# Attention product folded into the output weight, with the inverse denominators broadcast by DMA

## The chip, the cores and the metric

The kernel runs on one core of a Trainium2 chip. The metric is the device time of one execution in microseconds (us), as a median over several executions. "Span" is the time from the first to the last instruction in a profiled execution, about 2 us less than the device time.

The engines are called as in the profile: PE is TensorE's matmul, PEld its weight load, DVE is VectorE, ACT is ScalarE, POOL is GpSimd, SP is SyncE, and SPq is the queue of DMA instructions that SP issues. PSUM is the memory of the tiles that PE's matmuls write, such as `acc_t`. The granted clock is the share of its full clock that PE was given; 1.00 is full.

## The reference, cut to what matters

```python
def _A_ref(x, wqkv, wo):                      # S = 2048, D = 1024, 32 heads of 32
    q, k, v = ...                             # from x @ wqkv, split in heads
    phi = lambda t: jnp.where(t > 0, t + 1, jnp.exp(t)) + 1e-6
    pq, pk = phi(q), phi(k)
    kv = jnp.einsum("bhsd,bhse->bhde", pk, v)             # 32 x 32 per head
    z = jnp.einsum("bhsd->bhd", pk)
    num = jnp.einsum("bhqd,bhde->bhqe", pq, kv)
    den = jnp.einsum("bhqd,bhd->bhq", pq, z)[..., None] + 1e-6
    return (num / den).transpose(...).reshape(B, S, D) @ wo

h = x + _A_ref(_layernorm(x), A_wqkv, A_wo)
h2 = h + _B_ref(_layernorm(h), ...)           # the "mixer": two large products over S, 2048 -> 3584 -> 2048
```

Everything up to `h` takes the first 235 us of the kernel before. The mixer takes the rest, and the change does not touch its arithmetic.

## The kernel before

The stage in question has three parts. "Query units" compute q for 128 columns and 512 rows at a time and apply phi. Between them, for every block of 128 rows, numerator and denominator come from eight small products, are divided, and are transposed by DMA. Then the output projection multiplies with `wo`. Its PSUM tiles are not started at zero: ScalarE first copies the residual `x` into the tile (the "seed"), and PE accumulates on top.

```python
pin = tc.keep_in_program_order                # otherwise the compiler orders each engine's instructions
...
def attn_num_den(i):
    for j in range(ND):                       # ND = 8; L1118, PE
        nc.tensor.matmul(nd_ps[...], lhsT=pqT[:, j, i*P:(i+1)*P], rhs=ndrhs[:, j, :], start=True, stop=True)
    dn = ...; nc.scalar.activation(dn, nd_ps[...], ACT.Ln, bias=eps_den[:])      # L1126
    rd = ...; nc.scalar.activation(rd[:], dn[:], ACT.Exp, scale=-1.0)            # L1134
    for b in range(NNB):
        nc.vector.tensor_tensor(o_sb[...], nd_ps[...], rd[...], ALU.mult)        # L1139
    return o_sb

def attn_transpose(i, o_sb):
    nc.sync.dma_start_transpose(out=pqT[:, :, i*P:(i+1)*P], in_=o_sb[:])         # L1148
...
def load_xr(i):                               # residual rows, 4 tiles; SP queue
    xr = xrpool.tile([P, D], BF16, name="xr")
    nc.sync.dma_start(xr[:], x[i*P:(i+1)*P, :])                                  # L1154
    xrs[i] = xr

def out_proj(i):                              # i = 0..15, two halves of 512 columns
    ...
    for dc in range(NDC):
        ap_ = acc_tile()                      # ring of 5 PSUM tiles
        nc.scalar.copy(ap_[:, 0:CW], xr[:, dc*CW:(dc+1)*CW])                     # L1165, seed, ACT
        for j in range(ND):
            nc.tensor.matmul(ap_[:, 0:CW], lhsT=pqT[:, j, i*P:(i+1)*P], rhs=wo_sb[:, j, ...], ...)   # L1167
        nc.scalar.copy(h_bf[:, ...], ap_[:, 0:CW])                               # L1177, evacuation, ACT
        nc.vector.bn_stats(st[:, dc, :], ap_[:, 0:CW])                           # L1178, DVE
    nc.vector.bn_aggr(mv_all[:, i, :], st[:])
    nc.scalar.activation(lnv[:], mv_all[:, i, 1:2], ACT.Ln, ...)                 # L1181, statistics, ACT
    nc.scalar.activation(sc_all[:, i:i+1], lnv[:], ACT.Exp, scale=-0.5)          # L1182
    nc.sync.dma_start(h_dram[i][:], h_bf[:])
```

None of the instructions of `out_proj` is pinned: the compiler chooses the order in which ACT takes seeds, evacuations and statistics.

Of the kernel before, what the change touches and what calls it, by code (L numbers as in the profile page):

```python
# [27 lines left out]
def kernel(  # L28
# [28 lines left out]
    NCOL = P + HB  # L57
    JPB = BANK // NCOL
    NNB = (ND + JPB - 1) // JPB
# [40 lines left out]
    for q in range(HB):  # L100
        nc.vector.memset(maskbd[q * DH:(q + 1) * DH, q * DH:(q + 1) * DH], 1.0)
        nc.vector.memset(m4[q * DH:(q + 1) * DH, q:q + 1], 1.0)
# [5 lines left out]
    nc.vector.memset(eps_den[:], DEN_EPS)  # L108
# [27 lines left out]
    def load_w1(u, half):  # L136
        if half == 0:
            w1_tiles[u] = w_tile(wpool, WLEN)[:, 0:NS * CW].rearrange("p (k f) -> p k f", f=CW)
        k = slice(half * NSP, (half + 1) * NSP)
        nc.sync.dma_start(  # L140
            w1_tiles[u][:, k, :],
            B_w1[:, u * CW:(u + 1) * CW].rearrange("(k p) f -> p k f", p=P)[:, k, :],
        )
# [68 lines left out]
    class Inner:  # L212
# [7 lines left out]
        def sums(self):  # L220
            sm = [pools["is"].tile([P, self.nk, P], FP16, tag=self.tag, bufs=pools["is_bufs"], name="is")[:] for _ in range(4)]
            dve.tensor_tensor(sm[0], self.a21, self.a22, ALU.add)
# [196 lines left out]
    class Quad:  # L419
        def __init__(self, sts, mov1, mov5):  # L420
            self.sts = sts
            self.mov1, self.mov5 = mov1, mov5

# [19 lines left out]
        def pre(self, m):  # L443
            if m == 5 and self.mov1 is not None:
                self.in1 = Inner(self.sts, 1, self.mov1, "i1", self.sink1, self.sum1)
                self.in1.sums()
# [137 lines left out]
    with ExitStack() as actx:  # L584
        a3s = actx.enter_context(tc.tile_pool(name="a3s", bufs=4))
        a3w = actx.enter_context(tc.tile_pool(name="a3w", bufs=3))
        a3o = actx.enter_context(tc.tile_pool(name="a3o", bufs=3))
# [7 lines left out]
        ndrhs = pqpool.tile([P, ND, NCOL], BF16)  # L595
# [10 lines left out]
        with ExitStack() as a1:  # L606
# [476 lines left out]
            for n in range(3):  # L1083
                q_fill()
            for b in range(NKB):
                j0, n = b * KPB, min(KPB, ND - b * KPB)
                nc.vector.tensor_tensor(
                    ndrhs[:, j0:j0 + n, 0:P],
# [5 lines left out]
                    ndrhs[:, j0:j0 + n, P:NCOL],  # L1094
# [6 lines left out]
        warmctx.close()  # L1101
        wpool = sactx.enter_context(tc.tile_pool(name="wpool", bufs=2, side="right"))
# [7 lines left out]
        nd_ps = ndp.tile([P, NNB, BANK], F32, name="nd_ps")  # L1110
        nc.vector.memset(nd_ps[:], 0.0)

        with ExitStack() as a3:

            def attn_num_den(i):
                for j in range(ND):
                    b, sl = divmod(j, JPB)
                    nc.tensor.matmul(  # L1118
                        nd_ps[:, b, sl * NCOL:(sl + 1) * NCOL],
                        lhsT=pqT[:, j, i * P:(i + 1) * P],  # L1120
                        rhs=ndrhs[:, j, :],
                        start=True,
                        stop=True,
                    )
                dn = a3s.tile([P, NNB * JPB * HB], F32, name="dn")
                nc.scalar.activation(  # L1126
                    dn[:].rearrange("p (b s c) -> p b s c", b=NNB, c=HB),
                    nd_ps[:, :, 0:JPB * NCOL].rearrange("p b (s c) -> p b s c", c=NCOL)[:, :, :, P:NCOL],
                    ACT.Ln,
                    bias=eps_den[:],  # L1130
                    scale=1.0,
                )
                rd = a3s.tile([P, NNB * JPB * HB], F32, name="rd")
                nc.scalar.activation(rd[:], dn[:], ACT.Exp, scale=-1.0)  # L1134
                o_sb = a3o.tile([P, D], BF16, name="o_sb")
                for b in range(NNB):
                    nsl = min(JPB, ND - b * JPB)
                    blk = nd_ps[:, b, 0:nsl * NCOL].rearrange("p (s c) -> p s c", c=NCOL)
                    nc.vector.tensor_tensor(  # L1139
                        o_sb[:, b * JPB * P:(b * JPB + nsl) * P].rearrange("p (s h e) -> p s h e", h=HB, e=DH),  # L1140
                        blk[:, :, 0:P].rearrange("p s (h e) -> p s h e", e=DH),
                        rd[:, b * JPB * HB:(b * JPB + nsl) * HB].rearrange("p (s h) -> p s h", h=HB).unsqueeze(3).to_broadcast([P, nsl, HB, DH]),
                        ALU.mult,
                    )
                return o_sb

            def attn_transpose(i, o_sb):
                nc.sync.dma_start_transpose(out=pqT[:, :, i * P:(i + 1) * P], in_=o_sb[:])  # L1148
# [8 lines left out]
            def out_proj(i):  # L1157
# [4 lines left out]
                for dc in range(NDC):  # L1162
# [3 lines left out]
                    for j in range(ND):  # L1166
# [3 lines left out]
                            rhs=wo_sb[:, j, dc * CW:(dc + 1) * CW],  # L1170
# [23 lines left out]
            def attn(i):  # L1194
                attn_transpose(i, attn_num_den(i))

            TPC = SW // P
            for i in range(XRL):
                load_xr(i)
            for (u, j) in q_units[8:]:  # L1200
                q_unit(u, j)
                if u >= 1 and j % 2 == 1:
                    i = (u - 1) * TPC + j // 2
                    attn(i)
                    if i % 2 == 1 and i // 2 < 2:
                        load_wo(i // 2)
                    elif i % 2 == 1 and i // 2 < 6:
                        load_w1(*divmod(i // 2 - 2, 2))
            xctx.close()

# [6 lines left out]
            for i in range(NS):  # L1217
                if i % 2 == 0 and i // 2 < TPC:
                    attn(NS - TPC + i // 2)
# [46 lines left out]
    cur, nxt = nxt, quad1(1)  # L1266

# [126 lines left out]
```

## Time and profile before

| | before |
|---|---|
| time, median of 3 | 573.63 us (573.27 to 574.26) |
| span of the profiled run | 571.5 us |
| PE busy, DVE, ACT | 99%, 68%, 48% |
| share of PE in the chain that ended last | 95% |
| first and last matmul of the output projection | 178.14 and 235.20 us |

From the page of before, the busy times of the engines and the chain that ended last:

```profile
PE 563.7 (99%) x3124; PEld 293.3 (51%) x3124; DVE 390.2 (68%) x759; ACT 272.0 (48%) x585; POOL 1.8 (0%) x8
...
PE 95%; DVE 3%; ACT 1%; issue 1%; DMA 1%; ACTq 0%
```

PE is the limit nearly everywhere. The list of waits of before, for PE (columns: the waiting instruction, what it waited for, us in total, times, longest):

```profile
PE acc_t L94 <- DVE warm L86: 1.2, 1, 1.2
PE acc_t L674 <- ACT xnT L927: 0.7, 2, 0.4
PE psA L297 <- ACT psB L316: 0.7, 1, 0.7
...
PE psA L297 <- DVE hE L1189: 0.2, 1, 0.2
```

The two `psA` lines lie at the mixer's entry (237 to 240 us), and all others, also those left out, before 36 us. There is no line for the output projection (L1167): PE waits for nothing there. The table of windows of before says the same (columns: us, then busy us and instruction count of PE, PEld, DVE, ACT, POOL, the granted clock, DMA share, GB/s). The second window is the output projection, the third a steady stretch of the mixer's first product, counted as the 160 matmuls from the 1480th to the 1320th before the end:

```profile
120.00:178.14 58.14, 58.14 (x352) 29.88 (x351) 38.21 (x100) 37.12 (x83) 0.00 (x0) 1.00 0.62 157
178.14:235.20 57.06, 57.06 (x291) 26.73 (x288) 49.74 (x113) 40.12 (x100) 0.00 (x0) 1.00 0.57 150
305.74:332.89 27.15, 27.15 (x162) 15.64 (x160) 14.69 (x30) 14.10 (x31) 0.00 (x0) 1.00 0.25 78
```

PE is busy for all of each window. From the timeline of PE before (start, duration, engine, line, operation, tiles): a group of numerator products between query units.

```profile
158.07 0.63 PE L1118 MATMUL nd_ps<-ndrhs,pqT 128*128 128x132 bf16 x8
158.54 3.61 PE L1019 MATMUL acc_t<-xnT,wq_sb 128*128 128x512 bf16 x16
```

The next such group starts at 161.99, so from one to the next are 3.92 us. The 16 query matmuls between them take 16 x 0.216 = 3.45 us alone, so a group costs PE 0.47 us, and there are 16 groups.

### The profile page before, as it was taken

The page shows a single profiled execution, that of the slowest core. Times are in us where ns is not written, and L with a number is a line of the kernel's source. Part 1 is how long each engine was busy: PE and PEld are TensorE (multiplying, and loading weights), DVE is VectorE, ACT ScalarE, POOL GpSimd, SP SyncE. Part 2 cuts the span into 40 slices and gives each one's busy share as a digit, 9 for nine tenths or more (in the row PEclk, how much of TensorE's full clock was granted, in tenths as well). Part 3 has the DMA queues.
Part 4 walks back from the last instruction along what each step waited for, and adds up shares of the span by engine and source line. Part 5 has one row for each costly group of instructions (what it writes and reads, how often), then busy time and mean ns, then how long its engine had stood idle before and what let it go on. Part 6 is the DMA issues. An engine that isn't in the chain of part 4 may idle for free.

```text
span 571.5 us, 8308 instructions
## 1 busy us (share of the span) xinstructions
PE 563.7 (99%) x3124; PEld 293.3 (51%) x3124; DVE 390.2 (68%) x759; ACT 272.0 (48%) x585; POOL 1.8 (0%) x8
## 2 busy tenths in 40 slices
PE   7999999999999999999999999999999999999997
PEld 3444444455554444346555565555445655645643
DVE  6898887546767879873735627453979749659625
ACT  4747777666667776445445354453220411311211
POOL 1000000000000000000000000000000000000000
PEclk9999999999999999999999999999999999999999
DMA  9933432029536753104041340413892932912111
GB/s 303 357 76 79 89 74 38 19 96 323 118 72 127 177 178 111 55 2 147 1 148 28 120 148 1 148 48 81 205 255 84 244 96 75 278 56 73 38 47 46
DMA packets 97800, 66.61 MB, mean 117 GB/s; under 512 B 32082, under 2 KB 91744, under 8 KB 97760
## 3 DMA queue, kind: packets, MB, share of 16 engines
q1 hardware_dynamic: 97024, 65.42, 41.7%
q10 hardware_dynamic: 672, 0.66, 0.3%
q8 instruction: 24, 0.39, 0.3%
q14 instruction: 16, 0.13, 0.1%
q0 software_dynamic: 64, 0.01, 0.0%
HBM read 50.34 MB, written 8.39 MB: 103 GB/s over the span
## 4 chain that ended last, share of the span: by engine, by line
PE 95%; DVE 3%; ACT 1%; issue 1%; DMA 1%; ACTq 0%
PE psB L297 10%; PE psC L297 10%; PE acc_t L1019 9%; PE acc_t L1167 9%; PE psC L208 7%; PE psA L297 7%; PE psI L230 7%; PE psB L208 6%; PE psI L208 6%; PE psB L750 4%; PE psC L750 4%; PE psA L750 4%; PE psA L208 3%; PE acc_t L674 2%; PE psE L750 2%; PE psE L297 1%
## 5 line engine op out<-in xcount | busy, mean ns | idle before, releaser
L297 PEld LDWEIGHTS <-sa 128*128 128x128 f16 x436 | 42.6, 98 | 46.8 <-issue 0.7
L1019 PE MATMUL acc_t<-xnT,wq_sb 128*128 128x512 bf16 x256 | 58.0, 379 | 0.0
L1167 PE MATMUL acc_t<-wo_sb,pqT 128*128 128x512 bf16 x256 | 56.1, 379 | 0.0
L208 PEld LDWEIGHTS <-wq 128*128 128x128 bf16 (+1 forms) x357 | 34.5, 98 | 31.3
L297 PEld LDWEIGHTS <-wq 128*128 128x128 bf16 (+1 forms) x324 | 31.6, 98 | 33.1 <-issue 1.0
L208 PE MATMUL psC<-gs,wq 128*128 128x512 f16 (+2 forms) x210 | 45.0, 365 | 0.0
L1167 PEld LDWEIGHTS <-pqT 128*128 128x128 bf16 x256 | 24.8, 98 | 29.0
L1019 PEld LDWEIGHTS <-wq_sb 128*128 128x128 bf16 x256 | 24.5, 98 | 27.4
L166 ACT ACTIVATE e_sb<-acc_t 128x512 bf16<-128x512 f32 x40 | 23.9, 597 | 26.5 <-PE acc_t L1019 24.3
L170 DVE TENSOR_SCALAR e_sb<-e_sb 128x512 bf16<-128x512 bf16 x64 | 18.5, 289 | 25.4 <-ACT e_sb L166 24.8
L208 PEld LDWEIGHTS <-sa 128*128 128x128 f16 x231 | 22.6, 98 | 18.6
L750 PEld LDWEIGHTS <-xs 128*128 128x128 f16 x208 | 20.0, 98 | 23.3 <-DVE xs L736 1.3
L208 DVE TENSOR_TENSOR ot<-ot,hr 128x512 bf16<-128x512 bf16 (+2 forms) x27 | 11.2, 415 | 28.1 <-ACT ot L406 27.7
L333 ACT COPY psC<-psB 128x512 f32<-128x512 f32 x22 | 12.5, 570 | 35.1 <-PE psB L297 21.5
L297 PE MATMUL psB<-hT,sa 128*128 128x512 f16 x112 | 28.4, 379 | 0.0
L441 DVE TENSOR_TENSOR e<-psI,es 128x256 f32<-128x256 f32 x12 | 5.1, 425 | 34.0 <-PE psI L230 34.0
L297 PE MATMUL psC<-hT,wq 128*128 128x512 f16 x112 | 28.3, 379 | 0.0
L750 PE MATMUL psA<-wkv,xnT 128*128 128x512 bf16 x104 | 26.7, 379 | 0.0
L1178 DVE BATCH_NORM_STATS2 hst<-acc_t 128x6 f32<-128x512 f32 x32 | 22.1, 692 | 6.7 <-ACT h_bf L1177 6.5
L297 PE MATMUL psA<-hO,wq 128*128 128x512 f16 x112 | 25.6, 379 | 0.7 <-ACT psB L316 0.7
L297 PE MATMUL psB<-hO,sa 128*128 128x512 f16 x112 | 25.5, 379 | 0.0
L297 PE MATMUL psC<-hT,sa 128*128 128x512 f16 x112 | 25.5, 379 | 0.0
(184 smaller groups left out, 1022.9 us busy)
## 6 DMA issues: line engine op xcount, KB each, us to landing
wq<-in_B_w_dram SPq DMA_DIRECT2D x14, 1024.0 KB, 7.7
wq<-in_B_w_dram SPq DMA_DIRECT2D x8, 1792.0 KB, 9.1
xr<-in_A_x_dram SPq DMA_DIRECT2D x16, 256.0 KB, 3.1
h_dram<-h_bf SPq DMA_DIRECT2D x16, 256.0 KB, 2.2
hr<-h_dram SPq DMA_DIRECT2D x32, 128.0 KB, 2.4
out_dram<-ot SPq DMA_DIRECT2D x31, 128.0 KB, 1.8
x_sb<-in_A_x_dram SPq DMA_DIRECT2D x15, 256.0 KB, 3.2
wkv<-in_A_wqkv_dram SPq DMA_DIRECT2D x2, 1024.0 KB, 9.0
```

The lines of the kernel that those rows point to most:

```text
L166: pin(nc.scalar.activation(e_sb[:], src, ACT.Exp))
L170: pin(nc.vector.tensor_scalar(e_sb[:], e_sb[:], 1.0, PHI_EPS, ALU.min, ALU.add))
L208: return (lambda *a, **kw: pin(op(*a, **kw))) if Held.on else op
L230: pe.matmul(ps, lhsT=self.lhs[m][:, k, :], rhs=self.mov[m][:, k, :], start=(start and k == 0), stop=(k == self.nk - 1), skip_group_check=True,
L297: pe.matmul(ps[:, cols], lhsT=lhs[:, k, :], rhs=mv(k)[:, cols], start=(start and k == 0), stop=(k == self.nk - 1), skip_group_check=True,)
L333: nc.scalar.copy(self.C[:], self.B[:])
L441: dve.tensor_tensor(self.sts[m].e[:, self.cols(h)], ps, es, ALU.add)
L674: mm = nc.tensor.matmul(pp[:, 0:CW], lhsT=xnT[:, kt, i * P:(i + 1) * P], rhs=wkv[:, kt, c * CW:(c + 1) * CW], start=(kt == 0), stop=(kt == ...
L750: pin(nc.tensor.matmul(ps[:], lhsT=lhs[:, k, :], rhs=rhs[:, k, :], start=(start and k == 0), stop=(k == hk2 - 1), skip_group_check=True,))
L1019: nc.tensor.matmul(qp[:, 0:SW], lhsT=wq_sb[:, kt, j * P:(j + 1) * P], rhs=xnT[:, kt, u * SW:(u + 1) * SW], start=(kt == 0), stop=(kt == ND ...
L1167: nc.tensor.matmul(ap_[:, 0:CW], lhsT=pqT[:, j, i * P:(i + 1) * P], rhs=wo_sb[:, j, dc * CW:(dc + 1) * CW], start=(j == 0 and not SEED_RES ...
L1178: nc.vector.bn_stats(st[:, dc, :], ap_[:, 0:CW])
```

## The change

The intent is to take the numerator products off PE and the division off DVE. With K the block-diagonal kv, (pq K / den) wo is (pq / den)(K wo). So K is transposed on PE and multiplied once into `wo` ("fold"), the denominators are computed for 512 rows at a time with four column groups of the array side by side, and their inverse is written to DRAM and read back. One transfer per head row spreads that row over the 32 partitions of its head. DVE scales `pqT` with it.

```diff
-            def attn_num_den(i): ...          # 8 products 128x132, Ln, Exp, 3 DVE products, DMA transpose, 16 times
+            def kv_transpose():               # once
+                for j in range(ND):
+                    nc.tensor.transpose(tp[:, j, :], kvbd[:, j, :], ident[:])
+                nc.scalar.copy(kvT[:], tp[:])
+            def fold(j):                      # 8 times: wf = K wo, in place of wo
+                for c in range(NDC):
+                    nc.tensor.matmul(ps[:, 0:CW], lhsT=kvT[:, j, :], rhs=wo_sb[:, j, cols], start=True, stop=True)
+                    ...                       # copied to wf by ACT (c = 0) or DVE (c = 1)
+            def den(u):                       # 4 times
+                for o in range(2):
+                    for g in range(4):
+                        nc.tensor.matmul(ps[g * QR:(g + 1) * QR, :], lhsT=zz[:, j, ...], rhs=pqT[:, j, u * SW:(u + 1) * SW],
+                                         ..., tile_position=(0, g * QR))
+                nc.scalar.activation(ps[:], ps[:], ACT.Ln, bias=eps_den[:], scale=1.0 / S)
+                nc.scalar.activation(rd[:], ps[:], ACT.Exp, scale=-1.0)
+                pin(nc.sync.dma_start(rd_dram[u][:], rd[:]))
+                for h in range(2):
+                    for q in range(HB):
+                        pin(nc.sync.dma_start(rdb[q * DH:(q + 1) * DH, :, :],
+                                              rows[h, q].unsqueeze(0).to_broadcast([DH, 4, SW])))
+                    if 0 < u < 3:
+                        load_w1(u - 1, h, pin)
+            def scale_q(u, h):                # 8 times
+                pin(nc.vector.tensor_tensor(v, v, rdbs.pop((u, h))[:], ALU.mult))
...                                            # cut: tiles, call sites, pins; den(3) and the last four
...                                            # scale_q stand inside the loop of out_proj
```

More of the change, by code (lines that the diff above doesn't have):

```diff
@@ L56 @@
     HB = P // DH
-    NCOL = P + HB
-    JPB = BANK // NCOL
-    NNB = (ND + JPB - 1) // JPB
+    QR = P // 4
+    assert ND == 8 and 3 * HB <= QR
     KPB = BANK // (P + 1)
@@ L100 @@
     for q in range(HB):
-        nc.vector.memset(maskbd[q * DH:(q + 1) * DH, q * DH:(q + 1) * DH], 1.0)
+        nc.vector.memset(maskbd[q * DH:(q + 1) * DH, q * DH:(q + 1) * DH], 1.0 / S)
         nc.vector.memset(m4[q * DH:(q + 1) * DH, q:q + 1], 1.0)
@@ L107 @@
     eps_den = const.tile([P, 1], F32)
-    nc.vector.memset(eps_den[:], DEN_EPS)
+    nc.vector.memset(eps_den[:], DEN_EPS / S)
     b1_rows = const.tile([NF, P], BF16)
@@ L134, in w_tile, with load_w1 @@
         return pool.tile([P, n], BF16, tag="wq", name="wq")
-    def load_w1(u, half):
+    def load_w1(u, half, hold=lambda ins: ins):
         if half == 0:
@@ L139, in load_w1 @@
         k = slice(half * NSP, (half + 1) * NSP)
-        nc.sync.dma_start(
+        hold(nc.sync.dma_start(
             w1_tiles[u][:, k, :],
             B_w1[:, u * CW:(u + 1) * CW].rearrange("(k p) f -> p k f", p=P)[:, k, :],
-        )
+        ))
     def load_w2(p, pool):
@@ L218, in __init__, with sums @@
             self.lhs = {1: self.a11, 2: self.a12, 4: self.a22}
-        def sums(self):
+        def sums(self, hold=lambda ins: ins):
             sm = [pools["is"].tile([P, self.nk, P], FP16, tag=self.tag, bufs=pools["is_bufs"], name="is")[:] for _ in range(4)]
-            dve.tensor_tensor(sm[0], self.a21, self.a22, ALU.add)
+            hold(dve.tensor_tensor(sm[0], self.a21, self.a22, ALU.add))
             dve.tensor_tensor(sm[1], sm[0], self.a11, ALU.subtract)
@@ L422, in __init__ @@
             self.mov1, self.mov5 = mov1, mov5
+            self.hold = lambda ins: ins
         def cols(self, h):
@@ L445, in pre @@
                 self.in1 = Inner(self.sts, 1, self.mov1, "i1", self.sink1, self.sum1)
-                self.in1.sums()
+                self.in1.sums(self.hold)
             for st in self.sts:
@@ L585 @@
         a3s = actx.enter_context(tc.tile_pool(name="a3s", bufs=4))
-        a3w = actx.enter_context(tc.tile_pool(name="a3w", bufs=3))
-        a3o = actx.enter_context(tc.tile_pool(name="a3o", bufs=3))
+        a3d = actx.enter_context(tc.tile_pool(name="a3d", bufs=1))
         hstat = actx.enter_context(tc.tile_pool(name="hstat", bufs=1))
@@ L594 @@
         pqT = pqpool.tile([P, ND, S], BF16)
-        ndrhs = pqpool.tile([P, ND, NCOL], BF16)
+        kvbd = pqpool.tile([P, ND, P], BF16)
+        zz = pqpool.tile([P, ND, QR + HB], BF16)
         xctx = ExitStack()
@@ L1084 @@
                 q_fill()
+            nc.vector.memset(zz[:, :, 0:3 * HB], 0.0)
+            nc.vector.memset(zz[:, :, 3 * HB:], float(S))
             for b in range(NKB):
@@ L1087 @@
                 nc.vector.tensor_tensor(
-                    ndrhs[:, j0:j0 + n, 0:P],
+                    kvbd[:, j0:j0 + n, :],
                     kv_ps[b][:, 0:n, 0:P],
@@ L1093 @@
                 nc.vector.tensor_tensor(
-                    ndrhs[:, j0:j0 + n, P:NCOL],
+                    zz[:, j0:j0 + n, HB:2 * HB],
                     kv_ps[b][:, 0:n, P:P + 1].to_broadcast([P, n, HB]),
@@ L1101 @@
         warmctx.close()
+        kvT = xctx.enter_context(tc.tile_pool(name="kvtpool", bufs=1)).tile([P, ND, P], FP16, name="kvT")
         wpool = sactx.enter_context(tc.tile_pool(name="wpool", bufs=2, side="right"))
@@ L1109 @@
         ndp = a3p.enter_context(tc.tile_pool(name="ndp", bufs=1, space=PSUM))
-        nd_ps = ndp.tile([P, NNB, BANK], F32, name="nd_ps")
-        nc.vector.memset(nd_ps[:], 0.0)
+        rd_dram = [dram.tile([P, SW], FP16, name=f"rd_dram{u}") for u in range(NSC)]
         with ExitStack() as a3:
-            def attn_num_den(i):
+            def kv_transpose():
+                tp = ndp.tile([P, ND, P], BF16, tag="tp", name="kvtp")
                 for j in range(ND):
-                    b, sl = divmod(j, JPB)
-                    nc.tensor.matmul(
-                        nd_ps[:, b, sl * NCOL:(sl + 1) * NCOL],
-                        lhsT=pqT[:, j, i * P:(i + 1) * P],
-                        rhs=ndrhs[:, j, :],
-                        start=True,
-                        stop=True,
-                    )
-                dn = a3s.tile([P, NNB * JPB * HB], F32, name="dn")
-                nc.scalar.activation(
-                    dn[:].rearrange("p (b s c) -> p b s c", b=NNB, c=HB),
-                    nd_ps[:, :, 0:JPB * NCOL].rearrange("p b (s c) -> p b s c", c=NCOL)[:, :, :, P:NCOL],
-                    ACT.Ln,
-                    bias=eps_den[:],
-                    scale=1.0,
-                )
-                rd = a3s.tile([P, NNB * JPB * HB], F32, name="rd")
-                nc.scalar.activation(rd[:], dn[:], ACT.Exp, scale=-1.0)
-                o_sb = a3o.tile([P, D], BF16, name="o_sb")
-                for b in range(NNB):
-                    nsl = min(JPB, ND - b * JPB)
-                    blk = nd_ps[:, b, 0:nsl * NCOL].rearrange("p (s c) -> p s c", c=NCOL)
-                    nc.vector.tensor_tensor(
-                        o_sb[:, b * JPB * P:(b * JPB + nsl) * P].rearrange("p (s h e) -> p s h e", h=HB, e=DH),
-                        blk[:, :, 0:P].rearrange("p s (h e) -> p s h e", e=DH),
-                        rd[:, b * JPB * HB:(b * JPB + nsl) * HB].rearrange("p (s h) -> p s h", h=HB).unsqueeze(3).to_broadcast([P, nsl, HB, DH]),
-                        ALU.mult,
-                    )
-                return o_sb
-            def attn_transpose(i, o_sb):
-                nc.sync.dma_start_transpose(out=pqT[:, :, i * P:(i + 1) * P], in_=o_sb[:])
@@ new lines, in kv_transpose @@
+                    nc.tensor.transpose(tp[:, j, :], kvbd[:, j, :], ident[:])
+                nc.scalar.copy(kvT[:], tp[:])
+            wf = wo_sb[:].bitcast(FP16)
+            def fold(j):
+                for c in range(NDC):
+                    cols = slice(c * CW, (c + 1) * CW)
+                    ps = acc_tile()
+                    nc.tensor.matmul(ps[:, 0:CW], lhsT=kvT[:, j, :], rhs=wo_sb[:, j, cols], start=True, stop=True)
+                    if c == 0:
+                        nc.scalar.copy(wf[:, j, cols], ps[:, 0:CW])
+                    else:
+                        nc.vector.tensor_copy(wf[:, j, cols], ps[:, 0:CW])
@@ new lines @@
+            rds = {}
+            rdbs = {}
+            NH = ND // 2
+            def den(u):
+                ps = ndp.tile([P, SW], F32, tag="den", name="den_ps")
+                for o in range(2):
+                    for g in range(4):
+                        j = 4 * o + g
+                        nc.tensor.matmul(
+                            ps[g * QR:(g + 1) * QR, :],
+                            lhsT=zz[:, j, (1 - o) * HB:(1 - o) * HB + QR],
+                            rhs=pqT[:, j, u * SW:(u + 1) * SW],
+                            start=(o == 0),
+                            stop=(o == 1),
+                            skip_group_check=True,
+                            tile_position=(0, g * QR),
+                        )
+                rd = a3d.tile([P, SW], FP16, tag="rd", name="rd")
+                nc.scalar.activation(ps[:], ps[:], ACT.Ln, bias=eps_den[:], scale=1.0 / S)
+                nc.scalar.activation(rd[:], ps[:], ACT.Exp, scale=-1.0)
+                pin(nc.sync.dma_start(rd_dram[u][:], rd[:]))
+                for h in range(2):
+                    rdb = a3d.tile([P, NH, SW], FP16, tag="rdb", bufs=3, name="rdb")
+                    rows = rd_dram[u].rearrange("(g o h) n -> o h g n", g=4, h=HB)
+                    for q in range(HB):
+                        pin(nc.sync.dma_start(
+                            rdb[q * DH:(q + 1) * DH, :, :],
+                            rows[h, q].unsqueeze(0).to_broadcast([DH, 4, SW]),
+                        ))
+                    rdbs[u, h] = rdb
+                    if 0 < u < 3:
+                        load_w1(u - 1, h, pin)
@@ L1150 @@
+            def scale_q(u, h):
+                v = pqT[:, h * NH:(h + 1) * NH, u * SW:(u + 1) * SW]
+                pin(nc.vector.tensor_tensor(v, v, rdbs.pop((u, h))[:], ALU.mult))
             xrs = {}
@@ L1169, in out_proj @@
                             lhsT=pqT[:, j, i * P:(i + 1) * P],
-                            rhs=wo_sb[:, j, dc * CW:(dc + 1) * CW],
+                            rhs=wf[:, j, dc * CW:(dc + 1) * CW],
                             start=(j == 0 and not SEED_RESIDUAL),
@@ L1192, in normalize_h @@
                     combine(hE[:, q, :], hO[:, q, :], hT2[:, q, :], hT3[:, q, :], hT4[:, q, :])
-            def attn(i):
-                attn_transpose(i, attn_num_den(i))
             TPC = SW // P
+            for c in range(NDC):
+                load_wo(c)
             for i in range(XRL):
                 load_xr(i)
-            for (u, j) in q_units[8:]:
+            scale_at = {10: (0, 0), 13: (0, 1), 16: (1, 0), 19: (1, 1)}
+            for n, (u, j) in enumerate(q_units[8:]):
                 q_unit(u, j)
-                if u >= 1 and j % 2 == 1:
-                    i = (u - 1) * TPC + j // 2
-                    attn(i)
-                    if i % 2 == 1 and i // 2 < 2:
-                        load_wo(i // 2)
-                    elif i % 2 == 1 and i // 2 < 6:
-                        load_w1(*divmod(i // 2 - 2, 2))
+                if j == 0:
+                    den(u - 1)
+                if n == 1:
+                    kv_transpose()
+                if 4 <= n < 4 + ND:
+                    fold(n - 4)
+                if n in scale_at:
+                    scale_q(*scale_at[n])
             xctx.close()
+            a3w = a3.enter_context(tc.tile_pool(name="a3w", bufs=3))
             hpool = mctx.enter_context(tc.tile_pool(name="hpool", bufs=1, side="right"))
@@ L1217 @@
             for i in range(NS):
-                if i % 2 == 0 and i // 2 < TPC:
-                    attn(NS - TPC + i // 2)
+                if i == 0:
+                    den(NSC - 1)
+                elif i in (1, 3):
+                    scale_q(NSC - 2, i // 2)
+                elif i in (5, 7):
+                    scale_q(NSC - 1, i // 2 - 2)
                 if i + XRL < NS:
@@ L1266 @@
     cur, nxt = nxt, quad1(1)
+    nxt.hold = pin
     pend = run_pair(cur, pend, nxt, after1=sums1, after5=sums5)
```

## The prediction

> **What bounds the kernel now.** TensorE, almost everywhere. The page gives PE 99% busy. By the chain of waits 95% is PE. All PE waits in the list of waits sum to about 4 us, nearly all at the start (before 35 us) and at the entry to the first mixer (237 to 240 us: 0.15 us on DVE, 0.74 us on ACT). Between 126 and 235.5 us the table of windows gives PE 100% at full clock, while DVE is at 69 to 88% and ACT at 66 to 74%. So only PE's own work counts there.
>
> **What the change removes from PE.** The 128 numerator/denominator matmuls (128x132). In the timeline two query units (16 matmuls of 512 columns) take 3.45 us alone, but 3.92 us with one group of 8 such products: 0.47 us a group, 16 groups: **-7.5 us**. Off PE it removes 48 DVE products (23 us), 32 small ACT instructions, 16 DMA transposes.
>
> **What it adds to PE.**
> - Fold: 16 matmuls of 512 columns at the trace's spacing of 0.216 us: **+3.5 us**.
> - Eight 128x128 transposes, near the 0.058 us of the 132-column products: **+0.5 us**.
> - Denominators: 32 matmuls of 512 columns, 32 output rows each, in four column groups of the array. All four at once: 8 cost little over two passes, 0.43 us; serially 1.73 us. [...]I estimate 0.6 to 1.0 us each, four times: **+3.2 us** (6.9 us or more if serial).
> - New waits: each denominator group needs the last phi of its stretch. The trace shows ACT 1.1 us plus DVE 0.7 us after a unit's last matmul, and only one unit (1.73 us) now lies between, against two before. I estimate 0.1 to 0.3 us for the first three, about 0.7 us for the last, which is also split by output matmuls: **+1 us**.
>
> Sum: -7.5 +3.5 +0.5 +3.2 +1 = +0.7 us. The mixer's first products come in another order, which may recover some of the 0.9 us lost at its entry: I take -0.5 to -1.
>
> **Off the path.** Scaling: 8 DVE products of 2048 columns; the 3584-column ones take 2.02 us, so about 1.2 us each, 9 us against 23 us removed. The broadcasts: 32 DMAs of 128 KB; comparable ones (residual reads, 1 KB packets) landed in 2.4 us. From denominator to scaling lie 15 to 20 us; store 2.2 us, loads some 5 us, a 1 MB weight load between (7.7 us): they should land in time. The output weights landed by 131 us, the first fold is at some 141 us.
>
> **Prediction: 573.4 us, 571.0 to 577.0 (8 in 10). Faster by over 2%: 0.02; within 2%: 0.95; slower by over 2%: 0.03.**
>
> **What would show it.** Right: matmul count falls by 72; from the first denominator to the end of the output projection PE stays without gaps beyond about 0.5 us; a denominator group takes 0.6 to 1.0 us of PE between its neighbours; no DVE wait on the broadcast DMAs; DMA packets below 512 bytes fall by half or more. Wrong: denominators at 1.7 us or more a group (+4 us); DVE's scaling waiting for a broadcast[...].
>
> **What would make it wrong.** Column groups that don't overlap, or expensive switching of shape; broadcasts landing late behind weight loads in the one DMA queue; folds stalling the ring of five PSUM tiles because ACT is late with evacuations (1.77 us of work in 2.16 us of PE per unit).

No term of its sum is cut: -7.5 + 3.5 + 0.5 + 3.2 + 1 = +0.7 us, less 0.5 to 1 us for the mixer's entry. The 0.6 to 1.0 us for a denominator group (0.8, four times: the +3.2) stands as the author's estimate alone, between 2 x 0.216 = 0.43 us with all four at once and 8 x 0.216 = 1.73 us in series.

## The result, and the profile after

After: **580.99 us** median (579.33 to 582.01, 4 runs) against 573.45 us (573.16 to 574.26, 4 runs) for before. The ratio is 1.0126, with a 95% interval of 1.0100 to 1.0153. Ratios are the mean time of one kernel's runs over the mean of the other's in the same rounds, so they are not quite the ratio of the medians. The change of kernel is a slowdown of some 7 us. That is within 2%, as predicted, but above the predicted range.

The same two lines of the page, for after:

```profile
PE 565.7 (98%) x3052; PEld 288.7 (50%) x3052; DVE 383.2 (66%) x728; ACT 276.2 (48%) x570; POOL 1.8 (0%) x8
...
PE 75%; DVE 11%; DMA 7%; ACT 4%; issue 2%; SPq 1%; DVEq 0%; ACTq 0%
```

PE has as much work as before (565.7 us against 563.7), yet a quarter of the chain now runs through DVE, DMA and ACT. The list of waits of after, for PE, without the lines of the start:

```profile
PE acc_t L1190 <- ACT acc_t L1188: 3.7, 1, 3.7
...
PE acc_t L1190 <- DVE hst L1201: 1.2, 1, 1.2
...
PE psE L296 <- DVE hE L155: 0.6, 1, 0.6
PE psI L229 <- ACT psI L239: 0.4, 1, 0.4
PE psI L229 <- ACT psA L429: 0.4, 2, 0.2
```

L1190 is the output projection: it now loses 4.9 us. `psE` (L296) is at the mixer's entry. Both `psI` lines lie in the mixer, between 311 and 341 us; the list of before has none. Windows of after: up to the end of the long wait, after it, and the same 160 matmuls of the mixer.

```profile
194.00:202.15 8.15, 3.62 (x17) 1.56 (x17) 6.78 (x15) 3.98 (x11) 0.00 (x0) 1.00 0.76 243
202.15:207.50 5.35, 5.35 (x17) 2.05 (x17) 1.88 (x3) 3.21 (x7) 0.00 (x0) 0.68 0.37 98
311.43:340.18 28.75, 27.85 (x162) 15.63 (x160) 15.88 (x32) 14.31 (x32) 0.00 (x0) 1.00 0.23 74
```

There are three losses to see here. PE works 3.62 of the 8.15 us before 202.15. In the 5.35 us that follow, the granted clock is 0.68: 16 matmuls take 5.14 us, from start to start, instead of 3.45. (The expectation of e1 below says 1.9 us for this loss of 1.7, because it counts to the end of the last matmul.) And the mixer's 160 matmuls take 28.75 us instead of 27.15.

PE's own work is not the reason. Timeline of PE after, a denominator group and the transposes:

```profile
132.95 0.62 PE L1144 MATMUL den_ps<-pqT,zz 128*32 128x512 bf16 x8
133.50 1.90 PE L1019 MATMUL acc_t<-xnT,wq_sb 128*128 128x512 bf16 x8
135.24 0.61 PE L1120 MATMUL kvtp<-ident,kvbd 128*128 128x128 bf16 x8
135.68 0.59 PE L1019 MATMUL acc_t<-xnT,wq_sb 128*128 128x512 bf16 x2
```

From 132.95 to 133.50 are 0.55 us for eight matmuls of 512 columns. One after the other they would need 8 x 0.216 = 1.73 us, so the column groups gain a factor of 3.1. Counted between its neighbours a group costs 0.64 us, since its first matmul starts 0.31 us, and not 0.22, after the one before it; the factor is then 2.7. The transposes take 0.44 us.

Where the 7.4 us come from, by the start of the same matmul in both traces:

| point | before | after | lag |
|---|---|---|---|
| first matmul of the output projection | 178.14 | 179.22 | 1.1 |
| last matmul of the output projection | 235.20 | 241.60 | 6.4 |
| 1480th matmul before the end (mixer) | 305.74 | 311.43 | 5.7 |
| 1320th matmul before the end | 332.89 | 340.18 | 7.3 |
| last matmul | 568.06 | 575.45 | 7.4 |

So there are two separate losses: some 5 us of lag in the output projection (62.38 us from its first to its last matmul, against 55.64 in e11 below, which has the same products there and no wait above 0.2 us: 6.7 us lost), and 1.6 us in the steady part of the mixer, which the change does not touch. The first 1.1 us are no loss in themselves: the fold's matmuls now lie ahead of the projection, and the numerators no longer lie inside it.

**First loss: the output projection.** The timeline of ACT after, around the long wait (the bracket is idle time and what ended it):

```profile
196.73 0.59 ACT L1200 CAST h_bf<-acc_t 128x512 bf16<-128x512 f32 x1 [0.56 <-PE acc_t L1190]
198.46 0.59 ACT L1200 CAST h_bf<-acc_t 128x512 bf16<-128x512 f32 x1 [1.14 <-PE acc_t L1190]
201.08 0.29 ACT L1204 ACTIVATE hln_l<-mv_all,eps 128x1 f32<-128x1 f32 x1 [2.04 <-DVE mv_all L1202]
...
201.52 2.65 ACT L1188 CAST acc_t<-xr 128x512 f32<-128x512 bf16 x5
```

ACT evacuates two tiles (L1200), stands for 2.04 us at the statistics (L1204, waiting for DVE's `mv_all`), and only then writes five seeds in a row (L1188). (`mv_all` was late because DVE, busy without a gap from 196.21 to 201.05, had a normalization with its sums, two statistics and a scaling product ahead of it; so DVE's order has a share in the wait.) No seeded tile was left by then, so PE stood from 198.42 to 202.15 for the first seed. In this trace ACT started its instructions in the compiled order: from the first seed on its records follow the second line below, letter for letter (85), and for the 2.04 us no seed overtook the waiting L1204. So the order in which the compiler put them matters. The compiled order of ACT from the first seed on, read from the two builds (S seed, H evacuation, v statistics, q a query unit, D the inverse denominators; a listing, not a profile):

```
before  SSqSqDSSHSDHSDHSHvHSDSvHSHSvHSHDSHvSHHvSSHDSvHSHSvHSHSvHHSSvHHSSHvHSSvHHSSvHHSHSvSHvHHHvHv
after   SqqSSqSqSDHSHSvHSHHvHvHHSSvHHvSSSSSHSHSvHSHSvHHSSvHSHSvHHSHSvSHHSvSHHSvSHHSvSHHvHHvHv
```

In before, seeds and evacuations alternate. In after, `HHvHvHHSSvHHv` has two seeds to seven evacuations, and then come the five seeds at once. Why? The DMA instructions that SP issues, in the timeline of SP's queue after:

```profile
182.75 0.34 SPq L1156 DMA_DIRECT2D rd_dram<-rd  x1
...
184.51 0.42 SPq L1177 DMA_DIRECT2D xr<-in_A_x_dram  x1
...
188.49 3.72 SPq L1161 DMA_DIRECT2D rdb<-rd_dram  x8
192.26 0.43 SPq L1177 DMA_DIRECT2D xr<-in_A_x_dram  x1
```

The store of the last denominators, eight broadcasts and the residual loads `xr` stand in one queue. The eight broadcasts take 3.72 us of issue, and the residual load behind them starts at 192.26, 7.75 us after the one before. In before the loads come every 3 to 4.5 us from 176.37 on. Two readings are possible: the residual rows arrive too late on the chip, or the compiler, planning with this queue, wrote an ACT order with late seeds. The experiments have to tell, but this trace already speaks against the first. The load issued at 192.26 landed at 196.95 by its semaphore, 1.5 us before PE ran out of tiles; its first seed, which ends the long wait, began only at 201.52. And the list of waits of ACT, from 165 to 225 us of after, has no line for a residual load:

```profile
ACT acc_t L1188 <- DVE hst L1201: 6.9, 11, 0.9
ACT h_bf L1200 <- PE acc_t L1190: 4.8, 7, 1.2
ACT hln_l L1204 <- DVE mv_all L1202: 3.9, 3, 2.0
ACT e_sb L165 <- PE acc_t L1019: 2.6, 4, 0.6
ACT den_ps L1154 <- PE den_ps L1144: 0.4, 1, 0.4
```

**Second loss: the mixer.** There each window of work needs a weight block of 2 x 1 MB. The DMA view of before and of after, over the time of one such load (DMA: busy tenths in 40 slices; then GB/s in the same slices):

```profile
GB/s 23 129 140 181 246 158 181 339 374 380 404 398 380 386 386 374 386 374 363 351 334 357 357 334 363 339 363 345 345 345 351 339 351 363 334 351 269 129 53 6
...
q1 hardware_dynamic: 2080, 2.10, 93.9%
```

```profile
GB/s 44 78 88 258 254 176 346 385 380 390 390 390 385 390 361 366 341 356 346 356 336 361 341 346 366 336 424 317 336 332 263 88 20 10 10 24 20 24 20 10
...
q1 hardware_dynamic: 2080, 2.10, 77.9%
q8 instruction: 1, 0.02, 0.9%
```

In before the block takes 6.77 us (289.1 to 295.9). In after it takes 8.16 us (294.8 to 302.96), and the last eight slices of 0.21 us run at 10 to 24 GB/s, which is about one sixteenth, or less, of the some 380 GB/s before: it looks as if one of the 16 DMA engines finishes alone. The window of after holds one packet of another queue, q8 "instruction", and that of before holds none. Over the whole kernel q8 moves 24 packets of 16 KB (0.39 MB), one per 254 of PE's 6,104 instructions (matmuls and weight loads; in before also 24, one per 260); most of them take 0.9 to 1.4 us on their DMA engine. Below such a packet is called a fetch. That it brings PE's instructions is at this point a guess from the queue's name and the count. In before the fetch nearest to this load starts at 298.6 us, 2.7 us after the load's end; in after one starts at 300.2, inside the load. What this costs is what the experiments ask, because the change has 144 PE instructions fewer (72 matmuls, each with its weight load), which, if the guess holds, moves every later fetch against the weight loads.

### The profile page after: what moved, and what is told of

The parts are those of the page before. It is cut to its first block, busy times and chain, and to the rows that moved or that the text cites. A ratio compares the mean times of both kernels' runs of the same rounds, so it can differ in the third digit from the quotient of the medians.

```text
span 579.0 us, 8135 instructions
## 1 busy us (share of the span) xinstructions
PE 565.7 (98%) x3052; PEld 288.7 (50%) x3052; DVE 383.2 (66%) x728; ACT 276.2 (48%) x570; POOL 1.8 (0%) x8
## 4 chain that ended last, share of the span: by engine, by line
PE 75%; DVE 11%; DMA 7%; ACT 4%; issue 2%; SPq 1%; DVEq 0%; ACTq 0%
PE acc_t L1019 8%; PE psB L296 8%; PE psC L207 7%; PE psC L296 7%; PE psB L207 6%; PE psI L207 6%; PE psA L296 5%; PE psI L229 5%; PE psB L750 4%; PE psC L750 4%; PE psA L750 4%; PE psA L207 3%; DMA wq<-in_B_w_dram 3%; DVE hst L1201 2%; DMA rdb<-rd_dram 2%; PE psE L750 2%
## 5 line engine op out<-in xcount | busy, mean ns | idle before, releaser
L296 PEld LDWEIGHTS <-sa 128*128 128x128 f16 x436 | 42.6, 98 | 46.4
L1190 PE MATMUL acc_t<-wo_sb,pqT 128*128 128x512 f16 x256 | 57.6, 387 | 4.9 <-ACT acc_t L1188 3.7
L296 PEld LDWEIGHTS <-wq 128*128 128x128 bf16 (+1 forms) x324 | 31.7, 98 | 32.8 <-issue 0.9
L1190 PEld LDWEIGHTS <-pqT 128*128 128x128 bf16 x256 | 25.3, 99 | 37.1 <-issue 8.5
L296 PE MATMUL psB<-hT,sa 128*128 128x512 f16 x112 | 28.4, 379 | 0.0
L296 PE MATMUL psC<-hT,wq 128*128 128x512 f16 x112 | 28.3, 379 | 0.0
L296 PE MATMUL psA<-hO,wq 128*128 128x512 f16 x112 | 25.6, 379 | 0.0
L296 PE MATMUL psB<-hO,sa 128*128 128x512 f16 x112 | 25.5, 379 | 0.0
L296 PE MATMUL psC<-hT,sa 128*128 128x512 f16 x112 | 25.5, 379 | 0.0
```

The costliest lines, as they stand in the source:

```text
L296: pe.matmul(ps[:, cols], lhsT=lhs[:, k, :], rhs=mv(k)[:, cols], start=(start and k == 0), stop=(k == self.nk - 1), skip_group_check=True,)
L1190: nc.tensor.matmul(ap_[:, 0:CW], lhsT=pqT[:, j, i * P:(i + 1) * P], rhs=wf[:, j, dc * CW:(dc + 1) * CW], start=(j == 0 and not SEED_RESIDUAL),
```

## The experiments

All runs were correct unless it is said otherwise. Three theories stood at the start. A: the broadcasts, standing in SP's queue, delay or reorder what hangs on the residual loads. B: DVE's scaling products delay the releases of PSUM tiles. C: instruction fetches collide with the weight loads of the mixer.

### e1: broadcasts on the POOL queue

```diff
-                        pin(nc.sync.dma_start(
+                        pin(nc.gpsimd.dma_start(
                             rdb[q * DH:(q + 1) * DH, :, :],
```

> The 32 broadcast loads are issued from the POOL queue instead of the SP queue; nothing else is changed. Theory A (the broadcasts stand in the one in-order SP queue ahead of the residual loads xr, so the scheduler and the chip have the residual late, and the ScalarE seeds of the output banks with it): the TensorE waits of 1.2 and 3.7 us in the output projection vanish, with them the 1.9 us at a granted clock of 0.68 after them; time 572 to 575 us. Theory B (the scaling products, pinned in the VectorE order, hold up the statistics that free the PSUM banks): the waits stay, 579 to 582 us.

Measured: 576.60 us (576.26 to 577.95), ratio 1.0061 (1.0046 to 1.0077), against 573.22 us for before in the same rounds. PE's waits in the output projection are gone: it ends at 234.55, where the kernel before ends it at 235.20. The compiled ACT order has become regular again, though nothing but the queue of 32 DMAs differs (DVE's order changed with it, so e1 does not tell the two orders apart):

```
e1      SqqSSqSqSDHSHSvHSHHSvSHSvHHSHSSvHSHvSHHSSvHHSvSHSvHHSSvHHSSHvHSSvHHSSvHHSHSvSHvHHHvHv
```

The time missed the expectation upward, since the second loss stayed: the 160 matmuls of the mixer took 29.17 us. What follows: moving 32 DMAs to another queue takes away the first loss whole. The mixer's loss is independent of it.

### e2: the last four scaling products cut to 8 columns (wrong result)

```diff
-                v = pqT[:, h * NH:(h + 1) * NH, u * SW:(u + 1) * SW]
+                w = SW if u < NSC - 2 else 8
+                v = pqT[:, h * NH:(h + 1) * NH, u * SW:u * SW + w]
```

> The four scaling products that fall into the output projection (last two stretches) work on 8 of 512 columns a head row, so each has the same waits and place but costs about 0.1 instead of 1.2 us of VectorE. The result is wrong on purpose. Theory A: the order of ScalarE is the same as in the changed kernel and most of the wait stays; 577 to 581 us (at most the 1.2 us of the product that stands in the wait's chain is won). Theory B: both waits vanish, 572 to 575 us.

Measured: 580.31 us (579.79 to 580.86), ratio 1.0122 (1.0106 to 1.0137). The ACT order is that of after, letter for letter, and so is DVE's order. PE still waits 3.9 us for seeds, 1 us less than after. Theory B falls: 1 us of the first loss at most hangs on the scaling, and at the same granted clock (0.996 to 0.997) the time is 0.8 us less (580.3 us in the mean, against 581.1 for three runs of e4).

### e3: the residual loads on the POOL queue instead

```diff
-                nc.sync.dma_start(xr[:], x[i * P:(i + 1) * P, :])
+                (nc.gpsimd if i > XRL else nc.sync).dma_start(xr[:], x[i * P:(i + 1) * P, :])
```

> The residual loads from the fifth on are issued from the POOL queue, the broadcasts stay on SP: the victim is moved, not the blocker. Theory A: issue times of the residual loads move ahead from 184 to 200 us to about 177 to 190 us, TensorE waits in the output projection fall to less than 2 us in all, 572 to 577 us. Theory B: no change, 579 to 582 us.

Measured: 580.58 us (578.08 to 581.25), ratio 1.0118 (1.0093 to 1.0143): a miss. The residual loads no longer stand behind the broadcasts, and the wait in the output projection fell to 1.2 us. But the compiler again wrote an irregular order (`HHvSSHSvHHHHSHvSSvSHSSvHHHHHSvSS`), and PE waited 3.0 us at the mixer's entry, for DVE's `hE`. After that wait the clock was halved for 6.8 us (granted clock 0.69 from 239 to 250 us), which cost some 3 us more (an estimate: 5.9 us of PE work in it, at half speed). So most of the loss only moved. This was the first hint that the order, not the loads, is what costs.

### e4: the changed kernel once more

> The changed kernel unaltered, as a control on this chip: 579 to 582 us with the same two waits (1.2 and 3.7 us) in the output projection, if they come from the fixed order of instructions and not from chance; whether the 1.3 us lost between 306 and 333 us behind weight loads of the mixer is there again tells if that part is chance.

Measured: 581.08 us (579.80 to 581.23), ratio 1.0136 (1.0119 to 1.0153). The waits were the same, 3.7 and 1.2 us, and the mixer's stretch took 29.25 us: both losses repeat. The clock does not. This profiled run kept the full clock after the same 3.7 us wait (mean granted clock 1.000), where the first profile of after had half of it for 3.41 us (granted clock 0.50 from 202.55 to 205.96 us; PE was busy for 0.4 us of the 3.41 us before). e2 lost clock too (mean 0.996), and e3 (0.994), though their longest waits were only 2.7 and 3.0 us. So the length of the wait alone does not tell whether the clock falls. What does, these runs do not show. After's own runs lie in two groups as well, 579.3 to 579.8 at clock 1.0 and 580.8 to 582.0 below it.

### e5, e6 and e7: where PE's instruction fetches fall

e5 is after with 144 empty PE instructions put between early matmuls (28.7 to 70.2 us); the order on all engines is otherwise that of after. e6 adds the same to e1. e7 adds 112 to before: 112 more and 144 fewer lie 256 apart, about what passes from one fetch to the next by the counts above (254 and 260). So by estimate both move the fetches alike against the weight loads, and e7 should slow before as the change did.

```diff
+            nops = [144]                      # e7: 112
...
+                        if nops[0] > 0:
+                            nops[0] -= 1
+                            pin(nc.tensor.nop(hint=f"pad{nops[0]}", nofuse=True))
```

> The changed kernel with 144 empty instructions on TensorE's queue between the pinned products of the first projections[...]; the order of all other instructions on every engine is the same. TensorE's instruction count is again that of the kernel before. Theory C (the 16 KB instruction fetches[...] now fall inside the mixer's 1 MB weight loads, hold one of 16 DMA engines for 1.1 us, the load lands 1.4 us late and VectorE's sums with it): the fetches between 285 and 345 us are outside the weight bursts again, bursts last 6.6 to 6.9 us instead of 7.7 to 8.2, the waits between 306 and 340 us vanish, time 1.5 to 2.3 us below the changed kernel (578 to 579.6 us). The waits in the output projection stay. Rival (the later landing comes from chance or from the order of VectorE): no change, 580 to 582 us.

> Broadcasts on the POOL queue (e1) and the 144 empty instructions together. If theories A and C are the two causes and add: 573.5 to 575 us, nearly the kernel before; what is left is the mixer's entry. If not: 576 us or more.

> The kernel before with 112 empty TensorE instructions at the same place, so that its fetches stand to its weight loads as those of the changed kernel do[...]. Theory C: it becomes 1.5 to 2.3 us slower, 574.8 to 575.8 us, with waits of the mixer's first inner products at 300 to 335 us and bursts of 7.5 to 8.4 us. Rival: unchanged, 573 to 574 us.

Measured, against 573.26 us (9 runs) of before in the same rounds:

| run | time | ratio | 160 mixer matmuls | fetch inside the weight load of that stretch |
|---|---|---|---|---|
| before | 573.26 | | 27.15 us | no |
| e5: after + 144 | 578.55 (578.14 to 580.00) | 1.0094 (1.0079 to 1.0110) | 27.15 us | no |
| e6: e1 + 144 | 573.72 (573.61 to 573.89) | 1.0006 (0.9993 to 1.0018) | 27.15 us | no |
| e7: before + 112 | 575.46 (574.83 to 576.37) | 1.0041 (1.0027 to 1.0054) | 28.90 us | yes |

In these profiles and those of after, e1 and e4, the two weight loads of 2 MB that end between 290 and 330 us took 6.7 to 6.9 us where no fetch fell inside (before, e5, e6), and 7.7 to 8.4 us where one did (after, e1, e4, e7). The DMA view of e5 and e7 over the first of them:

```profile
q1 hardware_dynamic: 2080, 2.10, 51.7%
```

```profile
q1 hardware_dynamic: 2080, 2.10, 44.9%
q8 instruction: 1, 0.02, 0.5%
```

And what stands between the load and PE, in the list of waits of DVE over that stretch, in before, after and e7:

```profile
DVE is L222 <- DMA wq<-in_B_w_dram: 2.0, 1, 2.0
```

```profile
DVE is L221 <- DMA wq<-in_B_w_dram: 3.2, 1, 3.2
```

```profile
DVE is L222 <- DMA wq<-in_B_w_dram: 3.4, 1, 3.4
```

Theory C is shown, in both directions: adding work that does nothing speeds up one kernel by 2.4 us (0.0042 of 573, from the ratios of e4 and e5) and slows down the other by 2.2. The times of e4 and e5 also hold the chance of half clock; the profiles, at full clock there, do not. From the 1480th matmul before the end to the last they take 262.3 us in before, e5 and e6, 264.0 in after, 264.8 in e1 and e4, and 264.2 in e7. The weight block arrives 1.2 to 1.4 us later, DVE forms its sums later, then ACT, then PE. That the fetched instructions are PE's is inferred from the fact that padding PE alone moves the fetches, and from the count.

With e6 both losses are gone, and the changed kernel ties with before. The output projection ends 0.8 us earlier than in before (234.41 against 235.20), but this did not show: PE waited 1.8 us at the mixer's entry for DVE (`hE`).

### e8: e6 with the mixer's first sums earlier

```diff
-                if i == NS - 6:
+                if i == NS - 10:
                     cur = Mixer1(0)
```

> e6, and VectorE's eight sums for the mixer's first products are made from output tile 6 on instead of tile 10, where VectorE has idle time. In e1 VectorE is busy without a gap from 207 to 231 us and the last statistics start 1 us after their data. Expected: the wait at the mixer's entry falls from 2.0 us to about 1.2 us, 572.5 to 574 us; if VectorE's tail at the end is all latency, no change against e6.

Measured: 573.13 us (572.96 to 574.86), ratio 1.0003 (0.9989 to 1.0017). The wait at the entry is 1.3 us. A tie still.

### e9 and e10: seeds pinned, broadcasts in SP's queue

e9 leaves all DMAs in SP's queue and takes the compiler's freedom instead. It is e5 with seeds and evacuations pinned in alternation, seeds three tiles ahead. e10 adds the earlier sums of e8.

```diff
+            def seed_to(n):
+                for b in range(len(seeds), min(n + 1, NS * NDC)):
+                    seeds[b] = acc_tile()
+                    pin(nc.scalar.copy(seeds[b][:, 0:CW], xrs[b // NDC][:, ...]))
...
+                    seed_to(i * NDC + dc + AHEAD)            # AHEAD = 3
...
-                    nc.scalar.copy(h_bf[:, dc * CW:(dc + 1) * CW], ap_[:, 0:CW])
+                    pin(nc.scalar.copy(h_bf[:, dc * CW:(dc + 1) * CW], ap_[:, 0:CW]))
```

> e5 (the changed kernel, padded, all transfers on the SP queue) with ScalarE's copies of the residual into the output banks (seeds) and its evacuations held in a regular order, each seed three banks ahead of its products; broadcasts and residual loads stay in the SP queue. It tells apart two readings of theory A. If the fixed order of ScalarE, built at compile time around residual loads that it expected late, makes the waits: they vanish, 573.5 to 575 us. If the residual itself lands late on the chip: ScalarE then waits for the loads in order and TensorE behind it, 2 us or more of waits remain in the output projection, 576 to 579 us.

> e9 with VectorE's eight sums for the mixer's first products from output tile 6 on, as in e8. If e9 is right this is 572.5 to 574 us, at most 0.5 us under the kernel before: 0.6 us of TensorE work is saved before the mixer, and VectorE's tail at the mixer's entry takes it back unless the earlier sums shorten it.

Measured, against 573.06 us of before: e9 578.31 us (578.08 to 579.30), ratio 1.0089 (1.0070 to 1.0108); e10 578.37 us (577.50 to 579.45), ratio 1.0093 (1.0069 to 1.0117). Both missed. The number of e9 lies in the range foretold for rows that land late, but by luck. The long wait was gone; PE waited 2.9 us in seven pieces, and 1.4 us at the mixer's entry, and the list of ACT's waits of e9, in the output projection, says why:

```profile
ACT hln_l L1215 <- DVE mv_all L1213: 21.5, 15, 2.9
...
ACT acc_t L1190 <- DMA xr<-in_A_x_dram: 0.9, 1, 0.9
```

The residual load is late once, by 0.9 us. The rest is an error of the experiment: the statistics (`hln_l`) of each row block had come to stand directly behind its own evacuation and ahead of the next seed, and ACT waited for DVE there 15 times.

### e11 and e12: the statistics behind the next seed

e11 is e9 with the two small activations moved one output half later and pinned there. e12 is the same with the broadcasts on the POOL queue.

```diff
+                    if dc == 0 and i > 0:
+                        h_scale(i - 1)        # Ln and Exp of the statistics, pinned
```

```
e9      SqSqSDSHSHvSHSHvSHSHvSHSHv ...
e11     SqSqSDSHSHSHvSHSHvSHSHvSHSHv ...
```

> Kernel after with 144 empty TensorE instructions (no loss left in the mixer), broadcasts still in the SP queue, ScalarE's order in the output projection fixed as seed, evacuation, seed, evacuation, and the two small activations of the statistics moved one output half later, behind the next seed, so that they no longer wait for VectorE. Theory 'order' (what the output projection loses comes from the order that the compiler gave ScalarE because the residual loads stand late in the queue): TensorE waits in the output projection sum to under 0.8 us, ScalarE waits for residual loads at most about 1 us in all, time 573.0 to 575.0 us, ratio to before 1.000 to 1.003. Theory 'lateness' (the residual rows really arrive too late on the chip): ScalarE waits over 2 us for residual loads, TensorE loses 3 to 5 us in the output projection, time 576.5 to 579 us, ratio 1.006 to 1.010.

> As e11, with the broadcasts on the POOL queue. Theory 'order': within 1 us of e11, 572.5 to 574.0 us, since with a fixed ScalarE order the queue does not matter. Theory 'lateness': 3 to 4 us faster than e11. Either way this is the best form of the changed kernel known so far; it beats before only if VectorE's tail at the mixer's entry (1.8 us of TensorE wait in e6) shrinks below 1 us.

Measured, against 573.25 us (573.02 to 573.70, 9 runs) of before: e11 **572.61 us** (572.04 to 572.99, 5 runs), ratio 0.9988 (0.9974 to 1.0001); e12 **572.56 us** (572.44 to 572.77, 5 runs), ratio 0.9987 (0.9975 to 1.0000). The list of waits of e11, for PE after 170 us, is one line:

```profile
PE psE L296 <- DVE hE L155: 0.2, 1, 0.2
```

The queue of e11 is that of after. Here are its SP timeline and its waits of ACT:

```profile
182.53 0.34 SPq L1160 DMA_DIRECT2D rd_dram<-rd  x1
...
184.92 0.42 SPq L1181 DMA_DIRECT2D xr<-in_A_x_dram  x1
...
188.26 3.71 SPq L1165 DMA_DIRECT2D rdb<-rd_dram  x8
192.01 0.43 SPq L1181 DMA_DIRECT2D xr<-in_A_x_dram  x1
```

```profile
ACT hln_l L1222 <- DVE mv_all L1215: 6.4, 9, 1.6
...
ACT acc_t L1190 <- DMA xr<-in_A_x_dram: 1.8, 1, 1.8
```

The broadcasts stand in the same place, the residual loads are issued at the same times (184.92 and 192.01 against 184.51 and 192.26 in after), and the one late load even makes ACT wait 1.8 us (about 1 us was expected at most). It costs PE 0.18 us, because three tiles are seeded ahead. So the first loss was the compiled order, not the lateness: with the order fixed, the queue in which the broadcasts stand is worth 0.05 us. (The compiler also reordered DVE around the pinned ACT order, so after and e11 differ in both orders. Between e11 and e12 DVE's order differs in eight places, ACT's does not, and the time is the same. This speaks for ACT's order, but no run changes it alone.)

## Why the prediction was wrong

- **Work removed from PE, "-7.5 us", and added, "+3.5", "+0.5".** Right. Pieces measured in after: 0.43 us for two folds (3.45 in all), 0.44 for the transposes.
- **"Denominators ... 0.6 to 1.0 us each".** Right. Between its neighbours, as the prediction counts, each of the first three costs 0.64 us, and the last, split by output matmuls, 1.2: 3.1 in all against 3.2. Four side by side gave 3.1x (0.55 us against 1.73 in series), or 2.7x between neighbours.
- **"New waits ... +1 us".** Too high: the list of PE's waits in after has no line for the denominators (L1144). The corrected sum is -7.5 + 3.5 + 0.4 + 3.1 = -0.5 us; in e11, where nothing disturbs, the output projection ends 0.38 us before that of before (234.82 against 235.20).
- **"The mixer's first products come in another order, which may recover some of the 0.9 us lost at its entry".** Right in mechanism. In after the lag falls by 0.7 us there (6.4 to 5.7), but a kernel that comes late has less to wait for. In e11 the lead grows from 0.38 us at the end of the projection to 1.36 us at the 1480th matmul before the end, so 1.0 us is recovered. In e6 and e8 DVE's late work at the entry took it back.
- **The step that failed: "Off the path. ... they should land in time".** The broadcasts did land in time: no scaling product waited for one, in any profile. (Once it was close: in after one landed at 192.44, and DVE began to use it at 192.49.) But the step asked only whether they reach their own consumer. It did not ask what the new DMAs do to the rest of that queue's instructions and to the order that the compiler derives from them. What the runs showed in its place: an ACT order with the seeds behind evacuations and statistics, 4.9 us of PE waits, and in some runs 1.7 us or more from half clock after it. Together that is 5 to 7 us, against which stand the 0.4 us saved. e1, e11 and e12 each remove it in a different way.
- **"PE stays without gaps beyond about 0.5 us".** Wrong: gaps of 1.2 and 3.7 us. Its other signs came true: 72 matmuls fewer, no DVE wait on a broadcast, and packets below 512 bytes down from 32,082 to 15,762.
- **What the prediction left out: instruction fetches.** It counted 72 matmuls fewer as a gain only. The 144 fewer instructions moved the fetches into the mixer's weight loads: 1.6 us in the shown stretch of after, 2.4 us by e5, 2.2 us by e7.
- **"What would make it wrong".** Of the three named dangers none occurred: the column groups overlapped, the broadcasts were not late, and the folds did not stall the ring.

One thing stays open: why the compiler's order depends on the queue. That it does is shown: after and e1 differ in nothing but the queue of 32 transfers, and their ACT orders (and DVE's) differ. With the order left free, moving them won 4.5 us (medians of e1 and e4, same rounds; three of e4's four runs had lost some clock). That it reckons with the queue's issue time is argued, not shown.

## What to carry to other kernels

When a change adds transfers to a queue that others share (here eight took 3.72 us of issue ahead of a residual load), ask not only when they land, but what stands behind them, and compare the compiled order of every engine that feeds the critical one. The order can be built and read before anything runs. Where a tight loop lives from work done ahead (here seeds into five PSUM tiles), pin that order, and put small instructions that wait for another engine behind the work ahead (here 578.31 us in e9 became 572.61 in e11). When a stage that was not touched becomes slower, look at what else uses its DMA engines, and test with a few empty instructions before believing in a cause inside that stage (here 144 brought the mixer's stretch from 29.25 us in e4 back to 27.15 in e5).
